# Output weights as the last transfer, and output rows without transposes, in a decode kernel that streams a KV cache

## The chip, the core and the metric

The kernel runs on one core of one Trainium2 chip. The metric is the time of one execution in device microseconds (us). One execution of each kernel was also taken by the hardware profiler; its span, from first to last instruction, is about 1.8 us shorter than the time of that same execution. In the profile, PE is the matrix engine (PEld its weight loads), DVE the vector engine, ACT the scalar engine, POOL the general one, and SP the engine that issues most DMAs. By the profile's page the core has 16 DMA engines.

## The reference, cut to what matters

One token for a batch of two goes through attention over a cache and through an MLP; a gate mixes the two.

```python
x = A_x                                            # [2, 1, 1024], bf16
g = sigmoid((x * gate_w).sum(-1, keepdims=True))
# a: attention, H = 32 heads of 128, cache length 16384
q = (x @ wq) ...                                   # k_cache, v_cache: [2, 32, 16384, 128]
p = softmax(einsum("bhqd,bhkd->bhqk", q, k_cache) * 128 ** -0.5)
o = einsum("bhqk,bhkd->bhqd", p, v_cache)
a = o.reshape(2, 1, 4096) @ wo                     # wo: [4096, 1024]
# b: layer norm, gelu, w1, shifts, w2, residual x1, layer norm, w3, gelu, w4
b = x1 + gelu(layernorm(x1) @ w3) @ w4
return g * a + (1 - g) * b                         # [2, 1, 1024]
```

The two caches hold 128 tiles of 4 MB, one K and one V for each head and batch (537 MB); the weights that are loaded are about 34 MB, of which `wo` is 8.4 MB. With one token the shifts leave only zeros ahead of `w2`, so the kernels do not read `w1` and multiply `w2` by zeros.

## The kernel before

All loads go through a ring of five 32 KB slots per partition, in one order, on the SP queue. For each of the 64 head-and-batch pairs `g`, K is transposed in place on DVE and multiplied on PE, a softmax follows, and one step later V is multiplied (PV), copied out, extracted and normalised into column `g` of `OT_sb` [128, 64]. MLP weights are inserted in the order of loads at fixed `g`; their products run between the K products.

The output weights are two loads of 4 MB, one after half of the heads and one at `g` = 62. Partition `d` takes row `d` of every head, so a contiguous run is one row of 2 KB:

```python
def wo_rows(pi):
    h0 = pi * HPW                                   # HPW = 16 heads
    hn = min(HPW, H - h0)
    def fn(e, idx):
        src = A_wo[h0 * Dh:(h0 + hn) * Dh, :].rearrange("(h d) n -> d h n", d=Dh)
        return e.dma_start(ring[:, idx, 0:hn * D].rearrange("p (h n) -> p h n", h=hn), src)
    return fn
# [... cut ...]
def do_aproj(h):                                    # as soon as both columns of head h are there
    # [... cut ...]
    for nb in range(NBD):                           # weights stationary, two columns moving
        e.matmul(a_ps[:, nb, 0:2], lhsT=col4(wv, hl, nb), rhs=OT_sb[:, 2 * h:2 * h + 2], ...)
```

So the result stands in column form, [128, 8, 2], and the end of the kernel turns it into rows:

```python
for b in range(2):                                  # gate and mix, DVE
    e.scalar_tensor_tensor(outT_bf[:, :, b], a_ps[:, :, b], gT[:, b:b + 1], bgT_f[:, :, b], op0=ALU.mult, op1=ALU.add)
for nb in range(NBD):                               # eight transposes, PE
    e.transpose(o_ps[:, nb * P:(nb + 1) * P], outT_bf[:, nb, :], ident[:, :])
e.tensor_copy(xg_row[0:2, :].rearrange(...), o_ps.rearrange(...))   # two rows of 1024, DVE
e.dma_start(out[:, 0, :], xg_row[0:2, :])
```

## Time and profile before

| | before |
|---|---|
| time, median of 4 | 1348.68 us (1347.38 to 1349.61) |
| profiled execution | 1346.95 us, span 1345.2 |
| read from memory | 570 MB, 424 GB/s over the span |
| PE, DVE busy | 64%, 56% |
| last load (V) landed | 1336.1 us |
| from there to the end of the span | 9.1 us |

The end of the chain of waits in order of time (start us, length us, what):

```profile
1314.26 21.86 DMA ring<-in_A_v_cache_dram
1336.12 0.14 issue
1336.26 1.94 PE ps L593 x32
1338.20 0.02 issue
1338.22 0.61 ACT acc_sb L639
...
1339.44 0.44 PE ps L673 x8
...
1340.17 0.24 DVE outT_bf L713
...
1340.45 0.62 PE ps L719 x8
1341.07 0.02 issue
1341.10 2.41 DVE xg_row L722
```

After the last V everything is serial: PV (L593), the copy of its accumulator, the last head's `wo` product (L673), the mix, the transposes (L719), and a copy of only two partitions that takes 2.4 us (L722). The output DMA follows, to 1345.2.

Stretches of the kernel before (stretch, length; busy us and number of instructions of PE, PEld, DVE, ACT, POOL; granted PE clock; DMA share; GB/s):

```profile
680.00:720.00 40.00, 18.87 (x121) 7.46 (x118) 16.41 (x24) 2.75 (x6) 0.52 (x2) 0.74 1.02 418
1260.00:1300.00 40.00, 17.35 (x116) 6.84 (x115) 16.44 (x23) 2.75 (x6) 0.52 (x2) 0.75 1.00 410
1328.00:1332.00 4.00, 3.03 (x14) 1.15 (x12) 2.04 (x4) 0.00 (x0) 0.00 (x0) 1.00 0.61 258
1332.00:1336.00 4.00, 2.79 (x40) 1.39 (x40) 1.67 (x6) 1.38 (x3) 0.00 (x0) 1.00 0.31 131
```

The first two are the stretches after the `wo` loads, below the usual 431 GB/s. In the last two, before the last V has landed, the DMA share falls: some engines have finished and others have not. This is called the ragged end below.

### The profile page before, as it was taken

The numbers are of one execution on the slowest core, as the hardware profiler recorded it, in microseconds if no ns is written. First come the engines' busy times: TensorE is split into PE (matmuls) and PEld (weight loads), VectorE is DVE, ScalarE is ACT, GpSimd is POOL, SyncE is SP. The second block draws the span as 40 slices with busy tenths as digits, with TensorE's granted clock in tenths as the row PEclk, the third lists the DMA queues.
The fourth block names the chain that finished last, engine by engine and source line by source line (L and its number), as shares of the span: only waits on it lengthen the run. The fifth ranks groups of instructions, "written<-read, shape, count | busy, mean of one in ns | idle before, by whom it ended". The sixth has DMA issues, their size and how long they took to land.

```text
span 1345.2 us, 12862 instructions
## 1 busy us (share of the span) xinstructions
PE 864.8 (64%) x5666; PEld 347.8 (26%) x5666; DVE 757.0 (56%) x994; ACT 89.7 (7%) x195; POOL 23.3 (2%) x94
## 2 busy tenths in 40 slices
PE   2665776657756666666675766766666666667546
PEld 2222332223222222222222222222222222222223
DVE  0655446446656655665563655665655566556635
ACT  0000000000000000000000000000000000000000
POOL 1000000000000000000000000000000000000000
PEclk9878567687879879787876879787977887788868
DMA  9999999999999999999999999999999999999995
GB/s 404 426 430 433 429 430 425 434 430 431 430 431 428 433 431 429 432 430 432 432 413 432 432 430 431 432 432 428 433 431 430 431 431 430 433 430 432 415 423 255
DMA packets 24402, 571.26 MB, mean 425 GB/s; under 512 B 2197, under 2 KB 2197, under 8 KB 6298
## 3 DMA queue, kind: packets, MB, share of 16 engines
q1 hardware_dynamic: 24344, 570.44, 99.0%
q8 instruction: 44, 0.72, 0.2%
q14 instruction: 12, 0.10, 0.0%
q10 hardware_dynamic: 2, 0.00, 0.0%
HBM read 570.43 MB, written 0.00 MB: 424 GB/s over the span
## 4 chain that ended last, share of the span: by engine, by line
DMA 65%; PE 24%; DVE 10%; issue 1%; ACT 0%; POOL 0%; SPq 0%
DMA ring<-in_A_k_cache_dram 62%; PE ps L577 18%; DVE ring L565 7%; PE ps L593 3%; DMA ring<-in_A_wq_dram 2%; DMA ring<-in_A_v_cache_dram 2%; PE ps L400 1%; DVE rA L602 1%; PE ps L673 1%; DVE m_sb L614 0%; DVE OT_sb L660 0%; PE ps L609 0%; DVE rmax_bf L604 0%; PE ps L523 0%; PE ps L619 0%
## 5 line engine op out<-in xcount | busy, mean ns | idle before, releaser
L577 PE MATMUL ps<-ring,Z 128*128 128x512 bf16 x2048 | 661.9, 476 | 361.4 <-DVE ring L565 346.3
L565 DVE STREAM_TRANSPOSE ring<-ring 128x1024 f32<-128x1024 f32 x512 | 591.5, 1212 | 156.9 <-DMA ring<-in_A_k_cache_dram 156.9
L577 PEld LDWEIGHTS ps<-ring,Z 128*128 128x128 bf16 x2048 | 207.9, 113 | 714.3 <-DVE ring L565 447.1
L593 PE MATMUL ps<-ring,PT_sb 128*32 128x512 bf16 x2048 | 126.7, 391 | 0.6 <-DMA ring<-in_A_v_cache_dram 0.6
L630 ACT ACTIVATE P_sb<-ps,negm 128x512 bf16<-128x512 f32 x64 | 44.0, 687 | 1186.2 <-DVE negm L624 1186.2
L602 DVE TENSOR_REDUCE rA<-ps 128x1 f32<-128x512 f32 x64 | 44.3, 692 | 122.5 <-PE ps L577 122.5
L660 DVE TENSOR_SCALAR OT_sb<-ps,recip 128x1 bf16<-128x1 f32 x64 | 14.1, 221 | 153.5 <-PE ps L644 153.5
L636 DVE STREAM_TRANSPOSE PT_sb<-P_sb 128x512 bf16<-128x512 bf16 x64 | 45.6, 712 | 54.1 <-ACT P_sb L630 54.1
L593 PEld LDWEIGHTS ps<-ring,PT_sb 128*32 128x32 bf16 x2048 | 49.7, 98 | 46.3 <-issue 4.7
L609 PE MATMUL ps<-ident,rmax_bf 128*1 128x128 bf16 x64 | 14.0, 218 | 66.3 <-DVE rmax_bf L604 66.3
L639 ACT ACTIVATE acc_sb<-ps 128x512 bf16<-128x512 f32 x64 | 38.2, 597 | 55.4 <-PE ps L593 55.4
L558 POOL TENSOR_TENSOR Z<-q_f,mask 128x16 bf16<-128x16 f32 x64 | 16.6, 261 | 1217.4 <-PE ps L577 1197.0
L609 PEld LDWEIGHTS ps<-ident,rmax_bf 128*1 128x1 bf16 x64 | 5.1, 79 | 98.7 <-DVE rmax_bf L604 98.7
L614 DVE TENSOR_REDUCE m_sb<-ps 1x1 bf16<-1x128 bf16 x64 | 18.0, 281 | 19.9 <-PE ps L609 19.9
L644 PEld LDWEIGHTS ps<-dsel,acc_sb 128*128 128x128 bf16 x256 | 20.4, 118 | 33.3 <-issue 29.4
L624 DVE TENSOR_SCALAR negm<-ps,cAB 128x1 f32<-128x1 f32 x64 | 17.7, 277 | 17.3 <-PE ps L619 17.3
L651 PEld LDWEIGHTS ps<-rowsum,ones_f 128*128 128x128 f32 x128 | 19.2, 189 | 28.6 <-issue 27.3
L619 PE MATMUL ps<-m_sb,ones_bf 1*128 1x1 bf16 x64 | 11.1, 173 | 24.1 <-DVE m_sb L614 24.1
L651 PE MATMUL ps<-rowsum,ones_f 128*128 128x1 f32 x128 | 24.7, 262 | 1.2 <-ACT P_sb L630 1.2
L656 DVE RECIPROCAL recip<-ps 128x1 f32<-128x1 f32 x64 | 10.8, 169 | 24.4 <-PE ps L651 24.4
L523 PE MATMUL ps<-xT_bf,ring 128*128 128x2 bf16 x256 | 7.1, 165 | 18.2 <-DMA ring<-in_A_wq_dram 18.2
L644 PE MATMUL ps<-dsel,acc_sb 128*128 128x1 bf16 x256 | 17.5, 172 | 1.1 <-ACT acc_sb L639 1.1
(81 smaller groups left out, 125.5 us busy)
## 6 DMA issues: line engine op xcount, KB each, us to landing
ring<-in_A_k_cache_dram SPq DMA_DIRECT2D x64, 4096.0 KB, 41.1
ring<-in_A_v_cache_dram SPq DMA_DIRECT2D x64, 4096.0 KB, 35.5
ring<-in_A_wq_dram SPq DMA_DIRECT2D x2, 4096.0 KB, 17.5
ring<-in_A_wo_dram SPq DMA_DIRECT2D x2, 4096.0 KB, 43.3
ring<-in_B_w_dram SPq DMA_DIRECT2D x2, 3584.0 KB, 28.9
ring<-in_B_w_dram SPq DMA_DIRECT2D x1, 4096.0 KB, 34.1
ring<-in_B_w_dram SPq DMA_DIRECT2D x1, 3072.0 KB, 18.9
ring<-in_B_w_dram SPq DMA_DIRECT2D x1, 2048.0 KB, 41.5
```

Source lines behind the costliest of these rows:

```text
L565: ev_T[(g, u)] = pl.add("dve", lambda e: e.transpose(ap, ap), waits=(arrived(("k", g)),), sig=True)
L577: ev = pl.add("pe", lambda e, bp=bp: e.matmul(S_ps(pg)[:, 0:NCOL], lhsT=Z[:, pg, bp, ZO - 2 * u:ZO - 2 * u + P], rhs=kv[:, :, bp // 2, :, ...
L593: ev = pl.add("pe", lambda e, jj=jj, hf=hf, cg=cg: e.matmul(acc_ps[32 * cg:32 * cg + 32, 0:512], lhsT=PT_sb[:, pg, 32 * jj:32 * jj + 32], ...
L602: e1 = pl.add("dve", lambda e: e.tensor_reduce(rA[:, pg:pg + 1], S_ps(pg)[:, 0:NCOL], axis=AX.X, op=ALU.max), waits=(ev_S[g],), sig=True)
L609: ev_mt[g] = pl.add("pe", lambda e: e.transpose(mt_ps, rmax_bf[:, pg:pg + 1], ident[:, :]), waits=(ev_rmax[g], ev_m.get(g - 1), ev_ident) ...
L614: ev_m[g] = pl.add("dve", lambda e: e.tensor_reduce(m_sb[0:1, pg:pg + 1], mt_ps, axis=AX.X, op=ALU.max), waits=(ev_mt[g], ev_mb.get(g - 2) ...
L624: ev_negm[g] = pl.add("dve", lambda e: e.tensor_scalar(negm[:, pg:pg + 1], mb_ps, cAB[:, 0:1], cAB[:, 1:2], op0=ALU.mult, op1=ALU.add), wa ...
L630: ev_P[g] = pl.add("act", lambda e: e.activation(P_sb[:, pg, :], S_ps(pg)[:, 0:NCOL], ACT.Exp, bias=negm[:, pg:pg + 1], scale=scale, accum ...
L636: ev_PT[g] = pl.add("dve", lambda e: e.transpose(PT_sb[:, pg, :], P_sb[:, pg, :]), waits=(ev_P[g], ev_PV.get(g - 2)), sig=True)
L639: ev_accc[g] = pl.add("act", lambda e: e.activation(acc_sb[:, :], acc_ps[:, 0:512], ACT.Copy), waits=(ev_PV[g], ev_ext.get(g - 1)), sig=True)
L644: ev = pl.add("pe", lambda e, w=w: e.matmul(oT_ps, lhsT=acc_sb[:, w * P:(w + 1) * P], rhs=dsel[:, w:w + 1], start=(w == 0), stop=(w == 3)) ...
L651: ev_l[g] = pl.add("pe", lambda e: e.matmul(l_ps, lhsT=ones_f[:, :], rhs=rowsum[:, pg:pg + 1], start=True, stop=True), waits=(ev_P[g], ev_ ...
```

## The change

The intent: let the last bytes be those with the least work behind them. `wo` becomes the last transfer, so that all attention work runs under it; its last piece is small; and the product is formed as rows (two columns stationary, weights moving), so nothing needs transposing. The two halves of the columns go to two column groups of PE and stand on partitions 0, 1 and 32, 33. The MLP part is collected in the same rows. To read four rows per partition (8 KB runs), `OT_sb` is permuted once, by 16 small matmuls. The diff, cut to its core:

```diff
+        def wo_load(c0, cn, r0=0, rn=R4):
+            def fn(e, idx):
+                src = A_wo[c0 * R4 * P:(c0 + cn) * R4 * P, :].rearrange("(c p r) n -> p c r n", p=P, r=R4)[:, :, r0:r0 + rn, :]
+                return e.dma_start(wo_tile(idx)[:, c0 % CPS:c0 % CPS + cn, r0:r0 + rn, :], src)
+            return fn
 [... cut: the first slot is one load of 4 MB ...]
+                wloads[("wo", pi)] = [wo_load(k0, kn - 1), wo_load(k0 + kn - 1, 1, 0, 2), wo_load(k0 + kn - 1, 1, 2, 2)]   # 3, 0.5, 0.5 MB
 [... cut ...]
-            w_at.setdefault(g_load, []).append(("wo", pi))
 [... cut: after all K and V are queued ...]
+        for pi in range(len(wo_parts)):
+            q_load(("wo", pi))
 [... cut ...]
-        ev_x = pl.dma("sp", lambda e: e.dma_start(xg_row[0:2, :], A_x[:, 0, :]), s_misc)
+        ev_x = pl.dma("act", lambda e: e.dma_start(xg_row[0:2, :], A_x[:, 0, :]), s_misc)
 [... cut: w2 (once more) and w4 as row products into rows_ps; bgrow = (x + rows) * (1 - g) ...]
+        def do_aproj():
+            [... permute OT_sb to OT4_sb ...]
+            for (key, k), crs in wo_chunks:                      # waits for each piece
+                for c, r in crs:
+                    for hf in range(2):
+                        rows_ps[32*hf:32*hf+2, 0:512] += OT4_sb[:, r, c, :].T @ wt[:, c % CPS, r, hf*512:(hf+1)*512]   # tile_position (0, 32*hf)
 [... cut: transposes and two-row copy removed ...]
+                ev_fin = pl.add("dve", lambda e: e.scalar_tensor_tensor(orow[:, :], rows_ps[0:PR, 0:HD2], grow[0:PR, 0:1], bgrow[:, :], op0=ALU.mult, op1=ALU.add), ...)
+            ev_out = pl.dma(eng, lambda e: e.dma_start(out[:, 0, hf * HD2:(hf + 1) * HD2], orow[sl, :]), ...)   # halves on SP and ACT
```

(The accumulating matmul is written as a formula here; 336 matmuls fewer run in all.)

## The prediction

> **What bounds it now.** HBM transfers. The page gives 571 MB at a mean of 425 GB/s, and the slices show the DMA engines 9 tenths busy in every slice but the last; PE is 64% busy, DVE 56%, so neither limits. The chain of waits is 65% DMA. The time is therefore start + bytes/rate + whatever follows the last byte.
>
> **The tail now.** The chain in order of time ends: last V load landed 1336.1 us; PV 1.9, accumulator copy 0.6, extraction and OT 0.5, last head's w_o 0.44, two outT steps 0.5, eight transposes 0.6, copy of two rows 2.4 us, output DMA from 1343.5 to the end of the span at 1345.2 (1.7 us). That is 9.1 us with idle DMA engines.
>
> **What the change does.**
> 1. The last bytes are now w_o rows, not V. All attention work after the last V (about 4 us up to OT) runs under the last 8.4 MB (19.5 us at 430 GB/s, an estimate). After the last byte there remain: the last matmuls, one DVE step over 34x512, the output DMA. Transposes and the 2.4 us two-row copy vanish.
>    - Matmuls: the last three pieces (3, 0.5, 0.5 MB) hold 32 matmuls of 512 columns, in two column groups. From the timeline, a 512-column matmul comes every 0.22 us at full clock and 0.43 at half; two groups side by side give about 0.11 (four groups in PV: 0.06). So 32 take 3.5 us; they begin 2.4 us before the last byte: about 1.1 us stick out. At half clock about 4.4.
>    - DVE: 0.7 us (the 128x512 reduction out of PSUM takes 0.69).
>    - Output DMA 1.7, waits 0.1.
>    Tail about 3.7 us, 4.3 with some chance of the half clock: gain 4.8.
> 2. w_o now moves in 8 KB runs (4 KB in the last two) instead of 2 KB. By the windows, the two stretches after w_o issues ran below the usual 431: 408 and 429 GB/s (680 to 720 us), 396 and 424 (1260 to 1300): 1.2 and 1.9 us lost. [...] I expect 2.8 of the 3.1 us back.
> 3. The x load leaves the SP queue: the first w_q issue, at 1.15 us, comes 0.4 us earlier.
> 4. Off the path: w2 is multiplied once more in row form (16 matmuls), w4 in 56 wide matmuls instead of 224 narrow ones, 16 small permuting matmuls, a few constants. Loads take 35 to 41 us from issue to landing, four deep, so PE has slack for these: 0.
>
> The ragged end (DMA share 0.61 and 0.31 in the last 8 us before the last V landed; some engines finish early) should remain: total bytes are the same.
>
> **Sum.** -4.8 - 2.8 - 0.4 = -8.0 us: 1340.6 us, range 1336.5 to 1345. Faster by over 2% (27 us) would need more than the whole tail and is nearly excluded: 0.01. Within 2%: 0.98. Slower: 0.01.
>
> **What would show it.** The chain ends DMA w_o, a few row matmuls, one DVE step, output: 3.5 to 4.5 us after the last w_o landing, which comes near 1333. Middle slices without the 413 dip. PE idle before the first w_o piece lands.
>
> **What would make it wrong.** Granted clock: [...] here the clock was 0.50 from 1288 to 1308 after an idle stretch. PE waits some 5 us for w_o, so a cold end adds up to 3 us. Or the two column groups do not overlap (plus 3 us). Or the ragged end grows with small last transfers. Or the 2 KB loss had another cause.

Its sum is: -4.8 - 2.8 - 0.4 = -8.0 us, from 1348.6 to 1340.6.

## More of the kernel before

The page of the kernel before. The row of digits has the busy tenths of the DMA engines in 40 slices of the span, the next what they moved; the last line is the chain of waits by engine.

```profile
PE 864.8 (64%) x5666; PEld 347.8 (26%) x5666; DVE 757.0 (56%) x994; ACT 89.7 (7%) x195; POOL 23.3 (2%) x94
...
DMA  9999999999999999999999999999999999999995
GB/s 404 426 430 433 429 430 425 434 430 431 430 431 428 433 431 429 432 430 432 432 413 432 432 430 431 432 432 428 433 431 430 431 431 430 433 430 432 415 423 255
...
q8 instruction: 44, 0.72, 0.2%
...
DMA 65%; PE 24%; DVE 10%; issue 1%; ACT 0%; POOL 0%; SPq 0%
```

The DMA engines are the limit everywhere but in the last slice. The two dips (413, then 415 and 423) follow the two `wo` loads.

## The result, and the profile after

| | before | after |
|---|---|---|
| time, median of 4 | 1348.68 us | 1339.62 us (1339.60 to 1339.81) |
| span of the profiled execution | 1345.2 | 1338.0 |
| last load landed | 1336.1 | 1334.3 |
| from there to the end of the span | 9.1 | 3.7 |
| `wo` packets | 2 KB, 88 ns each | 8 KB, 314 ns each |

The ratio is 0.9934 with a 95% interval from 0.9917 to 0.9951. Ratios here are the mean time of one kernel's fast runs over that of the other's of the same rounds, so not quite the ratio of the medians quoted. By code the change lies within 2%; the gain of about 9 us is clear of the noise.

The page after:

```profile
DMA  9999999999999999999999999999999999999997
GB/s 407 427 433 432 428 434 421 436 428 432 431 433 428 431 433 430 433 430 432 430 433 429 432 429 433 429 433 431 431 432 431 433 429 432 431 432 432 428 431 304
...
q8 instruction: 42, 0.69, 0.2%
...
DMA 66%; PE 23%; DVE 10%; issue 1%; POOL 0%; SPq 0%; ACT 0%
```

The `wo` dips are gone (slices 21 and 38 to 39). The end of the chain after:

```profile
1290.90 40.88 DMA ring<-in_A_wo_dram
1331.78 0.04 issue
1331.83 3.66 PE ps L725 x32
1335.49 0.02 issue
1335.51 0.74 DVE orow L758
```

After the landing three steps remain (matmuls, a DVE step, output) where there were ten. Note what the chain names: not the last landing but that of the 3 MB piece, at 1331.78. The 32 matmuls of the last three pieces then run without a gap to 1335.49, while the last piece landed at 1334.3 (below). So PE sticks out by 1.2 us. PE alone, by the timeline (start, length, then idle time before it and what ended it):

```profile
1314.77 3.37 PE L638 MATMUL ps<-ring,PT_sb 128*32 128x512 bf16 x32 [2.69 <-DMA ring<-in_A_v_cache_dram]
...
1324.45 5.36 PE L725 MATMUL ps<-ring,OT_sb 128*2 128x512 bf16 x32 [4.74 <-DMA ring<-in_A_wo_dram]
1331.83 3.62 PE L725 MATMUL ps<-ring,OT_sb 128*2 128x512 bf16 x32 [2.02 <-DMA ring<-in_A_wo_dram]
```

The attention tail (the last PV, at 1314.77) lies under the `wo` transfers as intended. 32 matmuls took 5.4 us for the first slot, after 4.7 us of idle PE, and 3.6 us for the second. The stretches show why, in the column of the clock:

```profile
680.00:720.00 40.00, 27.10 (x155) 10.26 (x154) 24.43 (x31) 2.75 (x6) 0.52 (x2) 0.87 1.00 432
1260.00:1300.00 40.00, 25.07 (x144) 9.32 (x144) 24.48 (x31) 2.75 (x6) 0.26 (x1) 0.84 1.01 432
1324.00:1328.00 4.00, 3.55 (x18) 1.13 (x20) 0.00 (x0) 0.00 (x0) 0.00 (x0) 0.50 0.64 268
1328.00:1332.00 4.00, 1.98 (x20) 0.61 (x16) 0.00 (x0) 0.00 (x0) 0.00 (x0) 1.00 0.56 230
1332.00:1336.00 4.00, 3.44 (x32) 1.22 (x28) 0.49 (x1) 0.00 (x0) 0.00 (x0) 1.00 0.06 22
```

The clock was 0.50 for most of the first slot's matmuls and 1.00 from 1328 on, so for all of the last 32: the slow matmuls were off the path and the clock was back before those on it. The two stretches that used to hold the `wo` loads now run at 432 GB/s.

**The ragged end, seen closer.** In these two traces a load of 128 partitions counts its semaphore up 16 times, and the trace has the time of each count. They are read here as one count for each of the 16 DMA engines; the DMA share agrees, as after the seven early counts below it is 0.56 (changed kernel, 1328 to 1332), nine of 16. These are the sixteen counts of the last load of each kernel, in us (computed from the trace's semaphore records, on the profile's time axis):

```
before (V, 4 MB):    1329.0 1329.0 1329.2 1329.2 1329.3 1329.8 1329.9 | 1334.2 1334.4 1334.5 1334.6 1334.9 1336.0 1336.0 1336.1 1336.1
after (wo, 0.5 MB):  1324.7 1324.8 1324.9 1325.0 1325.6 1325.7 1326.0 | 1332.2 1332.2 1332.3 1332.5 1332.5 1332.8 1332.8 1332.9 1334.3
```

Seven engines are early, nine late. The gap grows over the whole run: in both traces the spread is 0.5 us for the first load and between 7 and 10 in the last 80 us. The time is set by the latest engine, not by the mean: the last count of the 3 MB piece stands at 1331.8, and its matmuls begin at 1331.83. Two questions follow: what makes engines late, and did the 2 KB runs cost the late ones anything?

### The profile page after: what moved, and what is told of

Read it like the earlier page. It is cut to its first block, busy times and chain, and to the rows that moved or that the text cites. A ratio compares the mean times of both kernels' runs of the same rounds, so it can differ in the third digit from the quotient of the medians.

```text
span 1338.0 us, 12205 instructions
## 1 busy us (share of the span) xinstructions
PE 851.6 (64%) x5330; PEld 329.4 (25%) x5330; DVE 757.8 (57%) x998; ACT 89.7 (7%) x195; POOL 24.1 (2%) x97
## 4 chain that ended last, share of the span: by engine, by line
DMA 66%; PE 23%; DVE 10%; issue 1%; POOL 0%; SPq 0%; ACT 0%
DMA ring<-in_A_k_cache_dram 62%; PE ps L622 17%; DVE ring L610 7%; DMA ring<-in_A_wo_dram 3%; PE ps L638 3%; DMA ring<-in_A_wq_dram 2%; DVE rA L647 1%; PE ps L456 1%; PE ps L427 1%; DVE m_sb L659 0%; DVE OT_sb L705 0%; PE ps L654 0%; DVE rmax_bf L649 0%; PE ps L725 0%; PE ps L664 0%
## 5 line engine op out<-in xcount | busy, mean ns | idle before, releaser
L622 PE MATMUL ps<-ring,Z 128*128 128x512 bf16 x2048 | 645.2, 466 | 361.1 <-DVE ring L610 345.2
L622 PEld LDWEIGHTS ps<-ring,Z 128*128 128x128 bf16 x2048 | 204.0, 111 | 719.4 <-DVE ring L610 461.8
L638 PE MATMUL ps<-ring,PT_sb 128*32 128x512 bf16 x2048 | 123.7, 384 | 2.7 <-DMA ring<-in_A_v_cache_dram 2.7
```

What stands on the lines that cost most here:

```text
L622: ev = pl.add("pe", lambda e, bp=bp: e.matmul(S_ps(pg)[:, 0:NCOL], lhsT=Z[:, pg, bp, ZO - 2 * u:ZO - 2 * u + P], rhs=kv[:, :, bp // 2, :, ...
L638: ev = pl.add("pe", lambda e, jj=jj, hf=hf, cg=cg: e.matmul(acc_ps[32 * cg:32 * cg + 32, 0:512], lhsT=PT_sb[:, pg, 32 * jj:32 * jj + 32], ...
```

## The experiments

Twelve kernels; the kernel before had medians of 1348.45, 1348.51 and 1348.10 us. All gave correct results unless stated.

**1. The yardstick.** The changed kernel unedited, beside the next three.

> The changed kernel once more, unedited, as the yardstick for the other runs of this call: 1339.6 us as before, span about 1338; last output-weight landing near 1334.3, then 3.7 us to the end of the span.

Measured: 1340.00 us (1339.72 to 1340.04), last landing 1334.5, 3.7 us before the end of the span. As expected, within 0.4 us.

**2. Row form, but V last.** The order undone, the form kept (the edit is shortened):

```diff
+            if g == G:                        # all wo loads ahead of the last V
+                for pi in range(len(wo_parts)): q_load(("wo", pi))
             if g - 1 < G: q_v(g - 1)
-        for pi in range(len(wo_parts)): q_load(("wo", pi))
-        ev_alast = do_aproj()
+        do_aproj(0, 7, ev_OT[G - 2])          # before the last PV: chunks of heads 0 to 27
+        ev_alast = do_aproj(7, 8, ev_OT[G - 1])   # after it: heads 28 to 31
```

> Row form kept, but the last V load is put back behind the output weights, and the output projection of all heads but the last four is done before it. If the tail is a plain sum of its steps, after the last V landing there remain PV 1.9, accumulator copy 0.6, extraction and OT 0.5, permutation 0.3 and its copy 0.25, eight matmuls 0.9, the DVE step 0.74, output 1.7 and waits 0.2: 7.1 us, against 3.7 with the weights last and 9.1 before the change. Time about 3.4 us over after_again, near 1343. Rival: the order of the last transfers does not matter because the row form alone brings the gain: time within 1 us of after_again.

Measured: 1345.66 us, 5.7 over the yardstick instead of 3.4. The last V landed at 1334.7, so the tail is 9.2 us, as long as before the change. PE in the timeline of this kernel:

```profile
1334.75 3.60 PE L639 MATMUL ps<-ring,PT_sb 128*32 128x512 bf16 x32 [9.47 <-DMA ring<-in_A_v_cache_dram]
...
1340.30 1.03 PE L728 MATMUL ps<-ring,OT_sb 128*2 128x512 bf16 x8 [0.36 <-DVE OT_sb L721]
```

PV took 3.6 us instead of 1.9, after 9.5 us of idle PE; the granted clock was 0.50 over 1332 to 1336 and 0.66 over 1336 to 1340 in this trace, and 1.00 under PV in the kernel before. The rival (the form alone brings the gain) falls: order is worth 5.7 us here, of which 1.7 is the slower PV.

**3. Order changed, old form.** From the kernel before: `wo` in eight loads of four heads, all at the end (shortened).

```diff
-    HPW = SLOT // D
+    HPW = 4
-            w_at.setdefault(g_load, []).append(("wo", pi))
+        for pi in range(NWO): q_load(("wo", pi))        # after all K and V
+            aproj_at.setdefault((G + 1, 4), []).extend(hs_)   # all products after the last OT
```

> The kernel before (column form, transposes, two-row copy, 2 KB runs) with only the order changed: output weights in eight loads of 1 MB as the last transfers. If the tail is a plain sum: after the last landing 32 narrow matmuls 1.35, two outT steps 0.5, transposes 0.6, copy 2.4, output 1.7, waits 0.2: 6.7 us. Time about 3 us over after_again plus whatever 2 KB runs cost (0 to 3 us): 1342.5 to 1346. Rival (only the row form helps): no better than the kernel before, 1348.

Measured: 1344.86 us, within the expected range. The end of its chain:

```profile
1336.03 0.05 issue
1336.07 1.24 PE ps L670 x32
...
1337.88 1.03 PE ps L716 x8
1338.91 0.02 issue
1338.93 2.41 DVE xg_row L719
```

The tail from the last landing (1336.0) to the end of the span (1343.0) is 7.0 us. The order alone brought 3.6 us over the kernel before, the form alone (experiment 2) 2.8, both 8.45. The two are not simply added: each alone leaves steps after the last byte that the other removes, the variant of this experiment still has 2 KB runs, and in both part of the tail was slower than before the change (PV in experiment 2, which began at a clock of 0.50; here the eight transposes, 1.03 us against 0.62, whose clock was not looked up).

**4. 2 KB runs at the end.** One row per partition, nothing else:

```diff
-  .rearrange("(c p r) n -> p c r n", p=P, r=R4)
+  .rearrange("(c r p) n -> p c r n", p=P, r=R4)
-  lhsT=OT4_sb[:, r, c, :]
+  lhsT=OT_sb[:, 2 * (R4 * c + r):2 * (R4 * c + r) + 2]
```

> The changed kernel with the output weights read in 2 KB runs (one row per partition and descriptor) and nothing else changed. The packets of the two traces took 88 ns for 2 KB and 314 for 8 KB, so 8.4 MB cost an engine 22.6 us instead of 20.1 if these durations follow each other: +2.5 us (the prediction's account, which read 3.1 us off the windows). Rival: the slower engines, which land last, lost only 0.75 us per 4 MB piece before the change (10.5 us between landings instead of 9.75): +1.2 to 1.5 us.

Measured: 1341.11 us (1340.86 to 1341.31), +1.1 against the yardstick: close to the rival's 1.2 to 1.5, far from the account's 2.5. The sixteen counts of the last load show where the rest went (the yardstick, then this kernel):

```
after_again: 1325.0 1325.0 1325.1 1325.2 1325.3 1325.5 1325.9 | 1332.4 1332.5 1332.5 1332.6 1332.7 1332.8 1332.8 1333.0 1334.5
wo_2k:       1329.3 1329.4 1329.5 1329.6 1329.7 1329.7 1329.8 | 1333.8 1333.8 1333.8 1334.0 1334.0 1334.0 1334.2 1334.4 1335.8
```

The early engines lost 4.3 us, the late ones 1.3. The mean over 16 engines, (7 x 4.3 + 9 x 1.3) / 16 = 2.6 us, is what the prediction had put down as the loss; but more than half of it fell on engines that had time to spare. Why the late engines lose less per byte than the early ones stays open.

**5. x back on SP.**

```diff
-        ev_x = pl.dma("act", lambda e: ...
+        ev_x = pl.dma("sp", lambda e: ...
```

> The load of x goes back to the SP queue ahead of the first weights; nothing else. The first weight issue moves from 0.74 back to about 1.15 us. Prediction's account: +0.4 us. Rival: the first landing is set by something else (the table load and other small transfers), 0.

Measured: 1339.98 us (1339.86 to 1340.09). The changed kernel had 1339.62 and 1340.00 us, and these differ by as much as the 0.4 us looked for. It was run at another time. The nearest kernel of the same call is that of experiment 9 (x on ACT, tiny loads added, a single run): 1340.07 us. So no gain from the earlier start is seen, but 0.4 us is at the limit of what these runs can tell. The first stretch did change; first the changed kernel, then this one:

```profile
0.00:5.00 5.00, 0.41 (x8) 0.33 (x8) 0.00 (x0) 0.00 (x0) 3.24 (x17) 1.00 0.72 256
```

```profile
0.00:5.00 5.00, 0.42 (x8) 0.34 (x8) 0.00 (x0) 0.00 (x0) 3.25 (x17) 1.00 0.63 211
```

So transfers do start earlier with x on ACT: 45 GB/s over 5 us is 0.2 MB, or about 0.5 us at 431 GB/s. At the end of this trace the typical late engine is 0.3 to 0.4 us later than in the yardstick, but the very last count stands at 1334.5 in both (1334.3 in the first trace of the changed kernel). The start was gained and did not visibly reach the time; with few traces the reason (one engine that lands last for another cause, experiment 8) is likely, not shown.

**6. Smaller pieces at the end.** The 3 MB piece as three of 1 MB, each with its own semaphore:

```diff
-  [wo_load(k0, kn - 1), wo_load(k0 + kn - 1, 1, 0, 2), wo_load(k0 + kn - 1, 1, 2, 2)]
+  [wo_load(k0 + i, 1) for i in range(kn - 1)] + [wo_load(k0 + kn - 1, 1, 0, 2), wo_load(k0 + kn - 1, 1, 2, 2)]
```

> The 3 MB piece of the last slot is loaded as three of 1 MB, each with its own semaphore, so that matmuls start with each. In the changed kernel the last 32 matmuls ran without a gap from the landing of the 3 MB piece at 1331.8 to 1335.5, while the last piece landed at 1334.3; if PE is what sticks out, only the last four matmuls remain after the landing (about 0.5 us instead of 1.2): -0.7 us. Rival: between pieces PE idles and its clock falls to half, the last matmuls take twice as long: -0.2 to 0.

Measured: 1339.42 us (1339.23 to 1339.47), 0.56 below experiment 5 and 0.65 below the single run of experiment 9. From its timeline:

```profile
1334.42 0.60 PE L726 MATMUL ps<-ring,OT_sb 128*2 128x512 bf16 x4 [0.56 <-DMA ring<-in_A_wo_dram]
1335.08 0.74 DVE L759 SCALAR_TENSOR_TENSOR orow<-ps,grow,bgrow 34x512 bf16<-34x512 f32 x1 [15.41 <-PE ps L726]
```

Now only four matmuls follow the last landing (1334.4). The clock was 1.00 under them, as in all of 1332 to 1336; before that it was 0.50 in 1324 to 1328 (shown in experiment 10), so the rival's cold end did not come about. This is a correct kernel a little faster than both given ones; against the changed kernel that rests on runs (1339.62 and 1340.00 us). They were run at other times.

**7. More PE instructions.** Between K products, where PE waits anyway:

```diff
+                if sc in (2, 6, 10, 14) and g < G:
+                    for i in range(4):
+                        e.matmul(banks[0][:, 300:301], lhsT=ones_bf[0:1, :], rhs=ones_bf[0:1, 0:1], start=True, stop=True)
```

> 1024 tiny matmuls more on PE (16 per head and batch, where PE waits for transposes anyway), 2048 PE instructions. Theory: half of the 16 DMA engines land about 8 us late at the end because the instruction fetches of PE (42 packets of 16 KB, about 1.06 us each, one per 256 PE instructions) fall on eight of them in turn; 8 more packets make each of these 1.1 to 1.3 us later: packets 42 to 50, spread of the landings 8.4 to 9.6, time +1.2 us. Rival: the engines differ in rate by themselves: more packets, but the same spread and time (0 to 0.2 us).

Measured: 1341.30 us, +1.3 against experiment 5. The line of the instruction queue, of this kernel:

```profile
q8 instruction: 50, 0.82, 0.2%
```

Eight packets more for 2048 PE instructions more, so one per 256 (in the changed kernel 42 for 10,660 matmuls and weight loads, one per 254), and the late engines alone moved (table below). The durations of such packets repeat roughly with a period of eight (in the changed kernel's trace, from the 15th packet on: 1016, 1018, 1072, 1069, 1060, 1108, 1107, 1086 ns, then 1016, 1026, ...), which fits eight engines in turn.

**8. Fewer PE instructions** (wrong result, relative error 0.024: the w3 and w2 column products are cut to one block each).

```diff
-                for nb in range(nout):
+                for nb in range(1):
```

> Wrong result on purpose: the narrow matmuls of the w3 and w2 products are cut to one in 28 and one in 8, 272 matmuls or 544 PE instructions fewer than the changed kernel; loads and everything else unchanged. Theory of fetches: PE packets fall from 42 to 40, five for each of eight engines instead of six for two of them; the one or two stragglers at the end (1.3 us after the others) vanish: time -1.3 us against the changed kernel (1339.6 to 1340.0). Rival: PE work, not fetches, was what more_pe slowed: cutting matmuls that lie off the critical path changes nothing.

Measured: 1338.50 us (1338.44 to 1338.57), 1.1 to 1.5 below the changed kernel. It was run at another time.

```profile
q8 instruction: 40, 0.66, 0.2%
```

The last load's counts by kernel:

(The three lines are from three chips; the changed kernel itself had 1339.62 and 1340.00 us.)

| kernel | PE packets | seven early engines | nine late engines | time |
|---|---|---|---|---|
| fewer_pe | 40 | 1324.9 to 1326.0 | 1330.7 to 1332.9 | 1338.50 |
| changed kernel (after_again) | 42 | 1325.0 to 1325.9 | 1332.4 to 1334.5 | 1340.00 |
| more_pe | 50 | 1324.8 to 1326.0 | 1332.9 to 1336.0 | 1341.30 |

The early engines do not move at all; the last of the late ones moves by 1.5 to 1.6 us per step. If eight engines take them in turn, 40 packets are five for each, 42 six for two of them, 50 seven for two. So what seems to count is the largest number that one engine gets.

The kept traces say more when the sixteen counts are followed from load to load (computed as above). In that of fewer_pe, 39 times an engine falls back by about 1.5 us (1.1 to 1.7), each time at a PE packet. Twelve smaller steps fall on the twelve packets of 8 KB of another instruction queue (q14): eight of 0.9 to 1.0 us, four of 0.3 to 0.6. There is no other step over 0.3 us. Five PE packets, 7.6 us, are the whole gap; so are the eight larger steps of q14, 7.7 us if they fall on one engine, which is then most likely the ninth late one (engines are not named in the records, so this is not shown). If a packet that begins after its engine is done costs nothing (read from these traces, not tested apart), the number of stragglers follows: the 40th of fewer_pe began at 1332.1, so one engine had only four and was done at 1330.7; the 42nd of after_again began at 1333.0, so one engine, not two, had six (1334.5); in experiment 6 it began at 1331.1, and two are last (1334.3 and 1334.4); the kernel before, with 44, has four (1336.0 to 1336.1).

That instruction fetches of PE make eight engines late is shown by these two runs in both directions and by the steps; the rival (the engines' own rates) falls, as they start within 0.5 us of each other. The cost is not hidden in this kernel, which is bound by DMA: each packet of 16 KB set one DMA engine back by about 1.5 us.

**9. Which engines are late.** Fourteen tiny loads of 2 to 15 rows behind `wo`, each with its own semaphore.

> The changed kernel with fourteen tiny loads of 2 to 15 rows queued behind the output weights on SP, each with its own semaphore, to see by their landing times which of the 16 engines are late. Theory of fetches: late engines are a fixed set, seven are early (about 8 us), in contiguous order or not. No expectation for the time (the kernel waits for the probes): within 1 us of the changed kernel.

Measured: 1340.07 us (a single run, so its state is unknown). A probe of n rows counts its semaphore up n + 1 times, once at once and then as often as it has rows (the loads of one and of two rows in the kernel before have 2 and 3 counts too). Going from one probe to the next shows which time was added:

```
rows  2: 1325.4 1326.3                                   3: + one at 1325-1326     4: + one at 1333.2
rows  5: + early      6: + late      7: + late      8: + early      9: + early     10 to 15: + late each time
```

If each probe ran on the engines of the one before and on one more (these times suggest it, the records name no engine), then, numbered in the order in which they were added, early are the engines 1, 2, 3, 5, 8 and 9, and, as seven are early in all and the first fifteen hold six, the 16th.

**10 and 11. Moving the last piece to early engines.** From experiment 6; the last 0.5 MB is cut by partitions, meant to run on three engines (the first three of the probe, all early), or, as a control, on five (of which the fourth was late in the probe). How many engines a piece of 123 or 125 partitions takes was assumption; the probe had 2 to 15 rows. The times expected of the control rest on it. The products of the moved piece are also done before those of the half piece in front of it:

```diff
-  wo_load(k0 + kn - 1, 1, 2, 2)                          # 128 partitions
+  *wo_few(k0 + kn - 1, 2, 2)                             # partitions 0:123, 123:126, 126:128; control 0:125, 125:128
```

> From split_tail: the last 0.5 MB piece is loaded as 123, 3 and 2 partitions instead of 128. [...] The probe's nested sets say the first three engines are early (done near 1325, the late ones near 1333 to 1334.4). If so, the late engines are relieved of 33 KB each: last landing 1334.4 to 1333.2, time -1.2 us against split_tail (1339.4), so about 1338.2. Rival: which engines are early differs from run to run, or three engines can't carry it in time: no gain or a loss.

> Control of balance3: the same piece as 125 and 3 partitions, [...] it ends near 1335.5, +1.1 us against split_tail, about 1340.5; 2.3 us over balance3. If the identity of the engines doesn't matter, balance5 is as fast as balance3 or faster [...].

Measured: 1342.56 us (1341.58 to 1342.94) and 1344.30 us: both slower than experiment 6 (1339.42, on another chip). The control is 1.7 us slower than the other, and in its trace one count of the moved piece stands at 1338.1 while all others were there by 1331.9, so a late engine did carry part of it; that there were five is not shown. But balancing failed. Two stretches, first of experiment 6, then of the one meant for three engines:

```profile
1324.00:1328.00 4.00, 3.46 (x18) 1.06 (x20) 0.00 (x0) 0.00 (x0) 0.00 (x0) 0.50 0.65 270
1328.00:1332.00 4.00, 4.00 (x36) 1.36 (x34) 0.00 (x0) 0.00 (x0) 0.00 (x0) 0.89 0.56 228
```

```profile
1324.00:1328.00 4.00, 3.54 (x18) 1.12 (x20) 0.00 (x0) 0.00 (x0) 0.00 (x0) 0.50 0.77 240
1328.00:1332.00 4.00, 3.30 (x30) 1.05 (x26) 0.00 (x0) 0.00 (x0) 0.00 (x0) 0.90 0.76 204
```

More engines were busy (0.77 against 0.65 in the first stretch; 0.76 against 0.56 in the second, so 12 against 9 of 16, an estimate from these shares that agrees with three more) and fewer bytes moved (240 against 270 GB/s). The 4 KB packets took 218 ns on average instead of 163, and the 1 MB pieces in front, which the late engines carry too, landed at 1327.7, 1331.7 and 1335.0 instead of 1326.9, 1329.4 and 1331.9; the moved piece itself landed at 1334.8 only. After the landing at 1335.0 sixteen matmuls took 3.1 us, where experiment 6 has four left at the end. So with the helpers busy the engines that they were to help got slower. Where the two meet is not shown by any run here.

**12. V last, with PE kept busy.** Experiment 2 with 26 unneeded matmuls of 512 columns ahead of the last PV:

```diff
+            if g == G:
+                for i in range(26):
+                    e.matmul(banks[3][:, 0:512], lhsT=ident[:, :], rhs=PermQ[...], start=True, stop=True)
```

> v_last with 26 unneeded matmuls of 512 columns while PE waits for the last V load. In v_last PV took 3.63 us after that landing against 1.91 before the change, and PE had been idle for about 8 us. If the halved clock after that idle time is what made the tail 9.2 us instead of the 7.1 expected, PV comes back to 1.9 and the time falls by 1.7 to 2 us, to about 1343.8. Rival: PV there is slow for another reason (DMA traffic into the same memory): no change.

Measured: 1344.34 us, but four runs from 1343.50 to 1346.26, where experiment 2 (on another chip) had 1345.02 to 1346.34. The profiled run was the slowest:

```profile
1325.81 4.91 PE L754 MATMUL ps<-PermQ,ident 128*128 128x512 bf16 x22
1334.47 3.61 PE L639 MATMUL ps<-ring,PT_sb 128*32 128x512 bf16 x32 [3.75 <-DMA ring<-in_A_v_cache_dram]
```

The filler ran at full clock (1.00 over 1324 to 1332), ended too early, and 3.75 us later PV was as slow as without it. So this run does not show the cure. That the clock was halved in the slow PV is read from the stretches of both traces (0.50 and 0.66 over 1332 to 1336, 0.66 and 0.50 over 1336 to 1340, for experiments 2 and 12); that filling the whole gap would bring back 1.7 us stays untested. In this trace the clock fell near 1333.3 (an estimate from the mean of 0.66 over 1332 to 1336), about 2.6 us after the last filler matmul on record.

## Why the prediction was right

The predicted 1340.6 us is 1 us from the measured 1339.62, and the range of 1336.5 to 1345 holds it. Point by point:

- **What bounds the kernel** was right: the DMA share stays at 9 tenths, and cutting or adding PE work off the path moved the time by what its instruction fetches cost (+1.3 us in experiment 7, -1.1 to -1.5 in experiment 8).
- **The tail, 9.1 to 3.7 us (4.3 with a chance of the half clock).** Right: 3.7 us from the last landing. PE sticking out by "about 1.1 us" measured 1.2, the DVE step 0.74 for 0.7, the output 1.7. The two column groups do run side by side: 32 matmuls of 512 columns took 3.6 us, where 22 on the whole array took 4.9 (the filler of experiment 12), both at a clock of 1.00. Since the clock was full at the end, the gain was 5.4 us, not 4.8. Experiment 6 confirms the 1.1 us: half of it can be had.
- **2 KB runs, 2.8 us.** Right in direction, not in size: 1.1 us in experiment 4. Four packets of 2 KB take 352 ns and one of 8 KB 314, so each packet more costs about 12.7 ns (an estimate from these durations). The prediction took the loss from GB/s, a mean over 16 engines; the time follows the late nine, which lost 1.3 us while the early seven lost 4.3.
- **x off the SP queue, 0.4 us.** The first stretch shows the earlier start, the time does not: no gain is seen in experiment 5, within the 0.4 us by which calls differ.
- **Off the path, 0.** Right for the products. A side effect was not foreseen: 672 PE instructions fewer (336 matmuls with their weight loads) make 42 fetch packets instead of 44. By the reading of experiment 8 it is worth nothing here, since the largest share of one engine stays six.
- **The ragged end "should remain".** Right: two groups of engines remain, with a spread of 9.6 us after, 7.2 before. The reason given, equal bytes, is not what makes the two groups: the fetches do (experiment 8).
- **Landing near 1333** was 1334.3; the two terms above, sized too large by 2.1 us together, are more than the difference.

The terms that came out smaller were partly made up for by the tail (0.6 us), and by the base: the profiled run of the kernel before, at 1346.95, was the fastest seen of it at that point, 1.6 us below the median of its other three runs (1348.58), from which the prediction subtracted. That the sum comes within 1 us of the result is therefore in part luck; order, form and tail are not. Between the spans of the two profiled runs the gain is 7.2 us, between the medians 9.1. The measured terms sum to 5.4 + 1.1 + 0 = 6.5 us, so 0.7 us of the profiled gain is assigned to nothing; experiment 4 also had all 2 KB runs at the end, where the kernel before had half of them in the middle. The kernel before varies by 2.7 us between runs (1346.95 to 1349.61), the changed one by 0.4. This goes with the order: the three kernels whose last load is V vary by 1.3 to 2.8 us, those that end with a whole `wo` piece by 0.1 to 0.5 (experiments 10 and 11 by 1.4 and 0.6). A PV that finds the clock halved in some runs and full in others would do this; that is not shown.

## What to carry to other kernels

In a kernel bound by transfers, order the loads so that the last one has the least work behind it, cut that load so that PE follows it piece by piece, and look at the clock that PE has when that load lands: here the products of the first `wo` slot ran just before and the last 32 matmuls found it at 1.00, while after 9.5 us of idle PE (experiment 2) it was 0.50 when V landed, and PV took 3.6 us instead of 1.9. Read a loss of bandwidth by engine before pricing it: the time follows the latest of the 16 DMA engines, and the 4.3 us that the early ones lost in experiment 4 did not reach it. PE instructions cost DMA time through their fetches: in these runs each packet of 256 set one engine back by about 1.5 us, and the time followed the engine with the most packets.
